# Rows of 512 elements for the gated activation, and 64 bytes between x and the weights in SBUF

## The chip, the cores and the metric

The kernel runs on one core of a Trainium2 chip. The metric is the device time of one execution in microseconds; before the change it is 534.3 us, the median of three runs (533.48 to 535.36). A measurement is compared with runs of the kernel before on the same chip.

## The reference

Banded attention over 8 images, 8 heads, 576 positions and 64 numbers per head; heads 0 to 3 see the last 32 positions, heads 4 to 7 every 32nd position. Its output, 4,608 tokens of 512 numbers, goes through a gated MLP. Cut to what matters here:

```python
h = np.maximum(x @ w_in, 0.0)                      # 4608 x 512 times 512 x 1024
hp = pad(h, 1 position on either side)
conv_out = sum(conv_w[k] * hp[:, k:k + S, :] for k in range(3))
gate = 1.0 / (1.0 + np.exp(-conv_out))
return (h * gate @ w_out)                          # 4608 x 1024 times 1024 x 512
```

## The kernel before

**Precision.** Both products of the MLP are made of three passes each: every operand is kept as a high and a low part (xh and xl, wih and wil, gh and gl, woh and wol, all of type fp32r), and high times high, high times low and low times high are added in PSUM. The weights arrive as 64-bit numbers and are taken apart on the chip in the first 85 us (`convert`, `from_f64`, lines 330 to 422).

**Tiling.** The 4,608 tokens are nine groups of N = 512 tokens (g = 0 to 8). The MLP works feature by feature: features lie on the 128 partitions, tokens along the row.

- `mm1` (line 607), the first product: for each of 8 blocks f of 128 hidden features it adds 4 blocks c of 128 inputs, three matmuls each (xh with wih, xh with wil, xl with wih). Every matmul streams a row of 512 tokens through a 128x128 block of weights: 96 matmuls in a group.
- `conv_gate` makes of the result, on ScalarE, VectorE and GpSimd, the gated activation of block f, and `split` (lines 430 to 435) stores it as the high part gh (ScalarE, line 431) and the low part gl (VectorE or GpSimd, line 434), in row f of two tiles of 8 rows.
- `mm2` (line 667), the second product: for each of 4 blocks m of 128 outputs it adds 8 blocks f, three matmuls each (woh with gh, wol with gh, woh with gl), 512 tokens wide: 96 in a group. The last group has one token more on its row (n = 513) and is done in two halves of 256 and 258 columns: 192 matmuls.

Between the matmuls of the MLP stand those of attention: scores (lines 449 and 458) and values (line 514) of four pairs of heads for every further image. The values of an image go into xh and xl, which hold 1,024 tokens, two groups, in 4 rows (c).

**Order.** All work is written down as operations with an engine, an expected duration, a due time and the keys that they read and write, in a `Plan`. `order` plays this plan through once, engine by engine, and the operations are then issued in the order found. The keys decide what waits in the plan: `("g", f)` with `"h"` or `"l"` stands for row f of gh or gl. On the chip, waits are set by the bytes that instructions touch.

**Layout.** The tiles of a pool lie one behind the other in SBUF in the order in which they are asked for, each at the next multiple of 32 bytes in every partition. The sizes per partition: xh, xl, wih, wil, woh and wol 16,384 bytes each (rows of 4,096 bytes for x and w_in, of 2,048 for w_out; a block of weights is 512 bytes wide), gh and gl 8 rows of N + 32 = 544 elements, 17,408 bytes. The attention buffers (qk, v, t, tt, mx, sm, twice) come behind wol, then the masks and smaller tiles.

Of the kernel before, what the change touches and what calls it, by code (L numbers as in the profile page):

```python
# [10 lines left out]
F32 = _mybir.dt.float32  # L11
F32R = _mybir.dt.float32r
BF16 = _mybir.dt.bfloat16
I32 = _mybir.dt.int32
# [6 lines left out]
P = 128  # L21
W = 32
# [42 lines left out]
class Plan:  # L65
# [6 lines left out]
    def op(self, engine, dur, at, fn, reads=(), writes=(), chain=(), table=None, lock=False, key=None):  # L72
        i = len(self.ops)
        deps = set(chain)
        for k in reads:
            if k in self.last_write:
                deps.add(self.last_write[k])
        for k in writes:
            deps.update(self.readers.get(k, ()))
            if k in self.last_write:  # L80
                deps.add(self.last_write[k])
        for k in reads:
            self.readers.setdefault(k, set()).add(i)
        for k in writes:
            self.last_write[k] = i
            self.readers[k] = set()
        deps.discard(i)
        self.ops.append((engine, dur, at, fn, deps, table, lock))
        return i
# [160 lines left out]
def tile_banded_attention_gated_mlp(ctx, tc, qkT, vw, w_in, conv, w_out, masks_in, picks_in, eye_in, out):  # L250
    nc = tc.nc
# [4 lines left out]
    NF, NM = w_in.shape[0], w_out.shape[0] // 2  # L256
# [4 lines left out]
    N = 4 * P  # L261
    NG = B * S // N
    HPS = [0, 2, 1, 3]
    V, A, G, T, Q = "dve", "act", "pool", "pe", "dma"
    plan = Plan()
    op = plan.op

    const = ctx.enter_context(tc.tile_pool(name="const", bufs=1))
    xh = const.tile([P, NC, 2 * N], F32R, name="xh")
    xl = const.tile([P, NC, 2 * N], F32R, name="xl")  # L270
    wih = const.tile([P, NC, FF], F32R, name="wih")
    wil = const.tile([P, NC, FF], F32R, name="wil")
    gh = const.tile([P, NF, N + 32], F32R, name="gh")
    gl = const.tile([P, NF, N + 32], F32R, name="gl")
    woh = const.tile([P, NF, DM], F32R, name="woh")
    wol = const.tile([P, NF, DM], F32R, name="wol")

    def attention_buffers(pool, i):
        qk = pool.tile([P, S + SP], F32, name=f"qk{i}")
# [5 lines left out]
    NB = 2  # L285
    buffers = [attention_buffers(const, i) for i in range(NB)]
    masks = const.tile([P, 2, 2, NBLK * 64], BF16, name="masks")
    picks = const.tile([P, 2, W], BF16, name="picks")
    eye = const.tile([P, P], F32, name="eye")
    eyer = const.tile([P, P], F32R, name="eyer")  # L290
    negr = const.tile([P, P], F32R, name="negr")
    cw = const.tile([P, 3 * NF], F32, name="cw")
    mlp = ctx.enter_context(tc.tile_pool(name="mlp", bufs=1))
    NHB, NPM = 3, 4
# [1 line left out]
    misc = mlp.tile([P, 2 * NHB * L], F32, name="misc")  # L296
    hs = [misc[:, L * i:L * i + L] for i in range(NHB)]
    cs = [misc[:, L * (NHB + i):L * (NHB + i) + L] for i in range(NHB)]
    carry = mlp.tile([P, NF, 2], F32, name="carry")
    psum = ctx.enter_context(tc.tile_pool(name="psum", bufs=1, space=PSUM))  # L300
    psR = psum.tile([P, 2048], F32, name="r")
    psM = [psum.tile([P, 512], F32, name=f"m{i}") for i in range(NPM)]
# [1 line left out]
    words = [const.tile([P, 8 * P, 2], I32, name=f"ws{i}") for i in range(NWS)]  # L304
    wa = [const.tile([P, 8 * P], I32, name=f"wa{i}") for i in range(NWA)]
    wl = [const.tile([P, 8 * P], F32R, name=f"wl{i}") for i in range(NWL)]
    small = const.tile([P, W], F32, name="small")
    diag = const.tile([P, 2 * NBLK, W], F32, name="diag")
    cwords = const.tile([P, 3 * NF, 2], I32, name="cwords")
    cwa = const.tile([P, 3 * NF], I32, name="cwa")  # L310
    cwt = const.tile([P, 3 * NF], I32, name="cwt")

# [114 lines left out]
        seen.add(a)  # L427
        return [("W", "in", b) for b in range(2)]

    def split(hi, lo, src, at, skey, key, e, ta, tv, tg, lock):  # L430
        op(A, ta, at, lambda: nc.scalar.copy(hi(), src), [skey], [(key, "h")])  # L431
        eng = nc.gpsimd if e == "p" else nc.vector
        op(G if e == "p" else V, tg if e == "p" else tv, at,
           lambda: eng.tensor_tensor(out=lo(), in0=src, in1=hi().bitcast(F32), op=ALU.subtract),  # L434
           [skey, (key, "h")], [(key, "l")], lock=lock or e == "p")

    def probabilities(n, at):
        i, hp = slot(n), HPS[n % NHP]
# [177 lines left out]
    def conv_gate(g, f, at, early, ps, kp):  # L616
        hi = state["h"] % NHB
        state["h"] += 1
        h, c_ = hs[hi], cs[hi]
        n = N + (g == NG - 1)  # L620
        cg = FIRST_CG if early else CG
        cut = 64 * g if 0 < g else None
        sg = FIRST_SPLIT_G[f] if early else SPLIT_G[f]
        op(A, 0.596, at + cg[2], lambda: nc.scalar.activation(out=h[:, 2:N + 2], in_=ps, func=AF.Relu), [kp], [("h", hi)])  # L624
        if g:
            op(G, 0.295, at + cg[0], lambda: nc.gpsimd.tensor_copy(out=h[:, 0:2], in_=carry[:, f, :]), [("carry", f)], [("h0", hi)], lock=True)  # L626
        if g < NG - 1:
            op(G, 0.3, at + cg[1], lambda: nc.gpsimd.tensor_copy(out=carry[:, f, :], in_=h[:, N:N + 2]), [("h", hi)], [("carry", f)], lock=True)
        kh = [("h", hi), ("h0", hi)]
        kc = ("c", hi)  # L630
        new = old(L * (NHB + hi), L)
        w0, w1, w2 = (cw[:, k * NF + f:k * NF + f + 1] for k in range(3))
        if not early or FIRST_SCALE[f] == "a":
            op(A, 0.725, at + cg[3], lambda: nc.scalar.activation(out=c_[:, :n], in_=h[:, 1:n + 1], func=AF.Copy, scale=w1),  # L634
               kh + ["cw"], [kc] + new)
        else:
            op(V, 0.4, at + cg[3], lambda: nc.vector.tensor_scalar(out=c_[:, :n], in0=h[:, 1:n + 1], scalar1=w1, scalar2=None,
                                                         op0=ALU.mult), kh + ["cw"], [kc] + new, lock=True)
        for k, wk in ((0, w0), (2, w2)):
            skip = n if cut is None else cut + 1 - k // 2  # L640
            for a, z in ((0, skip), (skip + 1, n)):
                if z > a:
                    op(V, 0.11 + 0.00117 * (z - a), at + cg[4] + 0.4 * k, lambda k=k, wk=wk, a=a, z=z: nc.vector.scalar_tensor_tensor(  # L643
                        out=c_[:, a:z], in0=h[:, a + k:z + k], scalar=wk, in1=c_[:, a:z],
                        op0=ALU.mult, op1=ALU.add), kh + [kc], [kc], lock=True)
        op(A, 0.63, at + cg[5], lambda: nc.scalar.activation(out=c_[:, :n], in_=c_[:, :n], func=AF.Sigmoid), [kc], [kc], table=1)  # L646
        ge = G if early and FIRST_GATE[f] == "p" else V
        op(ge, 0.69 if ge == V else 1.28, at + cg[6], lambda: (nc.vector if ge == V else nc.gpsimd).tensor_tensor(  # L648
            out=c_[:, :n], in0=h[:, 1:n + 1], in1=c_[:, :n], op=ALU.mult), kh + [kc], [kc], lock=True)
        split(lambda: gh[:, f, :n], lambda: gl[:, f, :n], c_[:, :n], at + cg[7], kc, ("g", f), sg, 0.62, 0.69, 1.2, True)  # L650

    def mm2(g, m, at):
        ms = slice(m * P, m * P + P)
        oi = (state["h"] + (0, 1, 2, 2)[m]) % NHB
        o, ko = (hs[oi], [("h", oi), ("h0", oi)]) if m == 2 else (cs[oi], [("c", oi)])
        cuts = [0, N] if g < NG - 1 else [0, N // 2, N + 1]
        first, last = N * g - 1, m == NM - 1
        for t, (a0, z) in enumerate(zip(cuts, cuts[1:])):
            x = z - a0 & 1
            mi = state["m"] % NPM  # L660
            state["m"] += 1
            ps = psM[mi][:, x:z - a0 + x]
            for f in range(NF):
                def products(f=f, ps=psM[mi][:, :z - a0 + x], tok=slice(a0 - x, z)):
                    n = 0
                    for a, y in ((woh, gh), (wol, gh), (woh, gl)):
                        nc.tensor.matmul(ps, a[:, f, ms], y[:, f, tok], start=(f == 0 and n == 0),  # L667
                                         stop=(f == NF - 1 and n == 2))
                        n += 1
                i = 2 * m + f // 4  # L670
                state["last"] = op(T, 0.697 if z - a0 == N else 0.36, at + 3 * t, products,
                                   [(("g", f), "h"), (("g", f), "l"), (("wo", i), "h"), (("wo", i), "l")], [("M", mi)], [])
            op(A, 0.59 if z - a0 == N else 0.38, at + 3 * t + 3, lambda ps=ps, a0=a0, z=z: nc.scalar.copy(o[:, a0:z], ps), [("M", mi)],  # L673
               ko)
            if g < NG - 1 or last:
                s = 1 if g == 0 else a0
                op(Q, 256 // len(cuts[1:]), at + 6, lambda s=s, z=z: nc.sync.dma_start(out=out[ms, first + s:first + z], in_=o[:, s:z]), ko, [])
        if g == NG - 1 and not last:
            op(Q, 256, at + 6, lambda: nc.sync.dma_start(out=out[ms, first:first + N + 1], in_=o[:, 0:N + 1]), ko, [])
# [8 lines left out]
    with tc.manual_schedule():  # L688
# [27 lines left out]
        for g in range(NG):  # L716
# [12 lines left out]
            if g + 1 < B:  # L729
                for j in range(NHP):  # L730
                    n = (g + 1) * NHP + j + 1
# [66 lines left out]
```

## Time and profile before

| what | us |
| --- | --- |
| median of three runs | 534.3 (533.48 to 535.36) |
| the profiled execution, its whole time | 535.48 |
| its span, first to last instruction | 533.3 |
| mean granted TensorE clock in it | 0.987 of full |
| TensorE in use | 511.3 |
| weight loads (PEld), beside it | 410.0 |
| VectorE, ScalarE, GpSimd in use | 362.4, 320.0, 118.8 |

The page gives times in us, and mean durations in ns. PE is TensorE's matmuls, PEld its weight loads. The duration of a matmul in the trace overlaps the next one's, so the time that one costs is read from start to start, or from a stretch of many in the chain of work that ended last. In that chain a row is the start, the length, the engine, what is written, the line, and the number of instructions.

### The profile page before, as it was taken

Reading aid. Unit: us, or ns where it says so; the run is one execution under the profiler, and the core shown is the slowest. Engines: PE = TensorE matmul, PEld = TensorE weight load, DVE = VectorE, ACT = ScalarE, POOL = GpSimd, SP = SyncE. Lnnn points to the kernel's source line nnn. Section 1 sums busy time; section 2 is a strip of 40 time slices with the busy share of each in tenths; the row PEclk is TensorE's granted clock in tenths of the full one; section 3 lists DMA queues with packets and bytes.
Section 4 is the critical chain, followed back from the end, with each engine's and each line's share of the span. In section 5 each row is a group of like instructions: output and inputs, shape, how many; then the busy total and the mean of one; then the engine's idle time right before and its main releaser. Section 6 shows DMA issues by size and latency. Waiting matters only on the chain.

```text
span 533.3 us, 16633 instructions
## 1 busy us (share of the span) xinstructions
PE 511.3 (96%) x7352; PEld 410.0 (77%) x7352; DVE 362.4 (68%) x639; ACT 320.0 (60%) x492; POOL 118.8 (22%) x197
## 2 busy tenths in 40 slices
PE   3787999999999999999999999999999999999997
PEld 3555677778877887788778877887788778888897
DVE  3967799866786568747975785688658845832840
ACT  2453786856674667556837776577547755733841
POOL 0111201532222112212131321222212221320210
PEclk9887999999999999999999999999999999999999
DMA  8655522343034403520334044303440101001001
GB/s 284 250 164 203 187 79 77 123 165 100 2 124 136 126 0 124 171 92 7 122 106 153 1 122 136 128 0 109 139 138 1 33 7 74 1 9 71 0 32 48
DMA packets 17639, 51.30 MB, mean 96 GB/s; under 512 B 2208, under 2 KB 3360, under 8 KB 17568
## 3 DMA queue, kind: packets, MB, share of 16 engines
q1 hardware_dynamic: 17568, 50.25, 28.0%
q8 instruction: 57, 0.93, 0.7%
q14 instruction: 14, 0.11, 0.1%
HBM read 40.80 MB, written 9.44 MB: 94 GB/s over the span
## 4 chain that ended last, share of the span: by engine, by line
PE 93%; ACT 2%; DVE 2%; DMA 1%; issue 1%; SPq 1%; ACTq 0%
PE m L667 39%; PE m L607 37%; PE r L514 6%; PE r L458 4%; PE m L411 2%; PE r L449 1%; DMA misc<-in_dram 1%; PE r L569 1%; PE m L412 1%; PE m L413 1%; ACT xh L549 0%; ACT wa L334 0%; ACT wih L400 0%; PE r L486 0%; DVE t L471 0%
## 5 line engine op out<-in xcount | busy, mean ns | idle before, releaser
L643 DVE SCALAR_TENSOR_TENSOR misc<-misc,cw 128x512 f32<-128x512 f32 (+29 forms) x256 | 127.9, 547 | 35.9 <-ACT misc L634 35.3
L667 PE MATMUL m<-gh,woh 128*128 128x512 f32 (+2 forms) x320 | 123.8, 387 | 0.0
L667 PE MATMUL m<-gl,woh 128*128 128x512 f32 (+2 forms) x320 | 118.8, 371 | 0.0
L667 PE MATMUL m<-gh,wol 128*128 128x512 f32 (+2 forms) x320 | 118.6, 371 | 0.0
L607 PE MATMUL m<-xh,wih 128*128 128x512 f32 x288 | 113.3, 393 | 0.0
L607 PE MATMUL m<-xh,wil 128*128 128x512 f32 x288 | 112.5, 391 | 0.0
L607 PE MATMUL m<-xl,wih 128*128 128x512 f32 x288 | 112.4, 390 | 0.0
L492 POOL TENSOR_TENSOR t<-t,sm 128x640 f32<-128x640 f32 x31 | 45.4, 1463 | 118.2 <-DVE sm L476 105.9
L667 PEld LDWEIGHTS m<-gh,woh 128*128 128x128 f32 x320 | 60.1, 188 | 12.4
L624 ACT ACTIVATE misc<-m 128x512 f32<-128x512 f32 x72 | 42.9, 596 | 43.2 <-PE m L607 41.5
L667 PEld LDWEIGHTS m<-gl,woh 128*128 128x128 f32 x320 | 60.1, 188 | 11.1
L667 PEld LDWEIGHTS m<-gh,wol 128*128 128x128 f32 x320 | 60.2, 188 | 9.1
L607 PEld LDWEIGHTS m<-xh,wih 128*128 128x128 f32 x288 | 54.1, 188 | 11.7 <-issue 0.2
L607 PEld LDWEIGHTS m<-xl,wih 128*128 128x128 f32 x288 | 54.2, 188 | 11.4
L607 PEld LDWEIGHTS m<-xh,wil 128*128 128x128 f32 x288 | 54.2, 188 | 11.3
L634 ACT ACTIVATE misc<-misc,cw 128x512 f32<-128x512 f32 (+1 forms) x70 | 50.6, 724 | 11.3 <-DVE gl L434 5.2
L648 DVE TENSOR_TENSOR misc<-misc 128x512 f32<-128x512 f32 (+1 forms) x69 | 47.8, 693 | 13.2 <-ACT misc L646 12.9
L646 ACT ACTIVATE misc<-misc 128x512 f32<-128x512 f32 (+1 forms) x72 | 44.6, 627 | 15.0 <-DVE misc L643 14.3
L431 ACT CAST gh<-misc 128x512 fp32r<-128x512 f32 (+1 forms) x72 | 44.2, 618 | 13.0 <-DVE misc L648 11.3
L673 ACT COPY misc<-m 128x512 f32<-128x512 f32 (+2 forms) x40 | 21.6, 546 | 47.9 <-PE m L667 47.3
L626 POOL COPY misc<-carry 128x2 f32<-128x2 f32 x64 | 19.1, 298 | 131.6 <-DVE misc L648 93.8
L470 DVE TENSOR_REDUCE mx<-r 128x10 f32<-128x640 f32 x32 | 26.3, 820 | 31.4 <-PE r L458 31.4
(84 smaller groups left out, 586.3 us busy)
## 6 DMA issues: line engine op xcount, KB each, us to landing
qk<-in_dram SPq DMA_DIRECT2D x32, 592.0 KB, 3.9
v<-in_dram SPq DMA_DIRECT2D x32, 384.0 KB, 3.4
ws<-in_dram SPq DMA_DIRECT2D x14, 512.0 KB, 4.7
out_dram<-misc SPq DMA_DIRECT2D x28, 256.0 KB, 3.1
misc<-in_dram SPq DMA_DIRECT2D x2, 512.0 KB, 5.8
out_dram<-misc SPq DMA_DIRECT2D x4, 255.5 KB, 3.7
out_dram<-misc SPq DMA_DIRECT2D x3, 256.5 KB, 2.0
masks<-in_dram SPq DMA_DIRECT2D x2, 160.0 KB, 2.6
```

The source lines that it names most:

```text
L431: op(A, ta, at, lambda: nc.scalar.copy(hi(), src), [skey], [(key, "h")])
L470: op(V, 0.826, at + offset[0], lambda: nc.vector.tensor_reduce(out=mx, in_=p3, axis=AX.X, op=ALU.max), ks, [("mx", i)])
L492: op(G, 1.28, at + offset[5], lambda: nc.gpsimd.tensor_tensor(out=t, in0=t, in1=sm.unsqueeze(2).to_broadcast([P, 2 * NBLK, 64]), op=ALU.mu ...
L514: nc.tensor.matmul(psV[64 * h:64 * h + 64, o:o + n_], v[W * c:W * c + W, h, j], tt[W * c:W * c + W, 64 * NBLK * h + a:64 * NBLK * h + z], ...
L607: nc.tensor.matmul(ps, a[:, c, fs], x[:, c, N * x0:N * x0 + N], start=(n == 0 and m == 0), stop=(n == NC - 1 and m == 2))
L624: op(A, 0.596, at + cg[2], lambda: nc.scalar.activation(out=h[:, 2:N + 2], in_=ps, func=AF.Relu), [kp], [("h", hi)])
L634: op(A, 0.725, at + cg[3], lambda: nc.scalar.activation(out=c_[:, :n], in_=h[:, 1:n + 1], func=AF.Copy, scale=w1), kh + ["cw"], [kc] + new)
L643: op(V, 0.11 + 0.00117 * (z - a), at + cg[4] + 0.4 * k, lambda k=k, wk=wk, a=a, z=z: nc.vector.scalar_tensor_tensor(out=c_[:, a:z], in0=h[ ...
L646: op(A, 0.63, at + cg[5], lambda: nc.scalar.activation(out=c_[:, :n], in_=c_[:, :n], func=AF.Sigmoid), [kc], [kc], table=1)
L648: op(ge, 0.69 if ge == V else 1.28, at + cg[6], lambda: (nc.vector if ge == V else nc.gpsimd).tensor_tensor(out=c_[:, :n], in0=h[:, 1:n + ...
L667: nc.tensor.matmul(ps, a[:, f, ms], y[:, f, tok], start=(f == 0 and n == 0), stop=(f == NF - 1 and n == 2))
L673: op(A, 0.59 if z - a0 == N else 0.38, at + 3 * t + 3, lambda ps=ps, a0=a0, z=z: nc.scalar.copy(o[:, a0:z], ps), [("M", mi)], ko)
```

## The change

It moves tiles in SBUF and changes the distance between rows of gh and gl. The operations of the first eight groups stay as they are.

- A row of gh and gl is 512 elements in all groups but the last, and 514 in the last one (`row`); the two become flat tiles of 8 x 514 elements, 16,448 bytes.
- carry, 64 bytes, is put between xl and wih. woh and wol go ahead of gh. Between gh and gl go eye, eyer, negr, picks, small and cwords, together 1,984 bytes.
- As a row of the last group overlaps two of the group before, its `split` also writes the key of row f + 1 in the plan (`over`).

Distances from the beginning of xh, in bytes per partition:

| tile | before | after |
| --- | --- | --- |
| xh, xl | 0, 16,384 | 0, 16,384 |
| carry | (behind misc) | 32,768 |
| wih, wil | 32,768, 49,152 | 32,832, 49,216 |
| gh, gl | 65,536, 82,944 | 98,368, 116,800 |
| woh, wol | 100,352, 116,736 | 65,600, 81,984 |
| first attention buffer | 133,120 | 133,248 |

```diff
     xh = const.tile([P, NC, 2 * N], F32R, name="xh")
     xl = const.tile([P, NC, 2 * N], F32R, name="xl")
+    carry = const.tile([P, NF, 2], F32, name="carry")
     wih = const.tile([P, NC, FF], F32R, name="wih")
     wil = const.tile([P, NC, FF], F32R, name="wil")
-    gh = const.tile([P, NF, N + 32], F32R, name="gh")
-    gl = const.tile([P, NF, N + 32], F32R, name="gl")
     woh = const.tile([P, NF, DM], F32R, name="woh")
     wol = const.tile([P, NF, DM], F32R, name="wol")
+    gh = const.tile([P, NF * (N + 2)], F32R, name="gh")
+    eye = const.tile([P, P], F32, name="eye")
+    eyer = const.tile([P, P], F32R, name="eyer")
+    negr = const.tile([P, P], F32R, name="negr")
+    picks = const.tile([P, 2, W], BF16, name="picks")
+    small = const.tile([P, W], F32, name="small")
+    cwords = const.tile([P, 3 * NF, 2], I32, name="cwords")
+    gl = const.tile([P, NF * (N + 2)], F32R, name="gl")
...
-    def split(hi, lo, src, at, skey, key, e, ta, tv, tg, lock):
-        op(A, ta, at, lambda: nc.scalar.copy(hi(), src), [skey], [(key, "h")])
+    def split(hi, lo, src, at, skey, key, e, ta, tv, tg, lock, over):
+        op(A, ta, at, lambda: nc.scalar.copy(hi(), src), [skey], [(k, "h") for k in [key] + over])
         eng = nc.gpsimd if e == "p" else nc.vector
         op(G if e == "p" else V, tg if e == "p" else tv, at,
            lambda: eng.tensor_tensor(out=lo(), in0=src, in1=hi().bitcast(F32), op=ALU.subtract),
-           [skey, (key, "h")], [(key, "l")], lock=lock or e == "p")
+           [skey, (key, "h")], [(k, "l") for k in [key] + over], lock=lock or e == "p")
...
-        split(lambda: gh[:, f, :n], lambda: gl[:, f, :n], c_[:, :n], at + cg[7], kc, ("g", f), sg, 0.62, 0.69, 1.2, True)
+        over = [("g", f + 1)] if n > N and f + 1 < NF else []
+        split(lambda: row(gh, g, f)[:, :n], lambda: row(gl, g, f)[:, :n], c_[:, :n], at + cg[7], kc, ("g", f), sg, 0.62, 0.69, 1.2, True, over)
+
+    def row(y, g, f):
+        pitch = N if g < NG - 1 else N + 2
+        return y[:, pitch * f:pitch * f + pitch]
...
-                        nc.tensor.matmul(ps, a[:, f, ms], y[:, f, tok], start=(f == 0 and n == 0),
+                        nc.tensor.matmul(ps, a[:, f, ms], row(y, g, f)[:, tok], start=(f == 0 and n == 0),
```

The other lines of the diff take the moved tiles out of their old places.

More of the change, by code (lines that the diff above doesn't have):

```diff
@@ L287, in tile_banded_attention_gated_mlp @@
     masks = const.tile([P, 2, 2, NBLK * 64], BF16, name="masks")
[L288 to L291, printed above, removed]
     cw = const.tile([P, 3 * NF], F32, name="cw")
@@ L298, in tile_banded_attention_gated_mlp @@
     cs = [misc[:, L * (NHB + i):L * (NHB + i) + L] for i in range(NHB)]
-    carry = mlp.tile([P, NF, 2], F32, name="carry")
     psum = ctx.enter_context(tc.tile_pool(name="psum", bufs=1, space=PSUM))
@@ L306, in tile_banded_attention_gated_mlp @@
     wl = [const.tile([P, 8 * P], F32R, name=f"wl{i}") for i in range(NWL)]
-    small = const.tile([P, W], F32, name="small")
     diag = const.tile([P, 2 * NBLK, W], F32, name="diag")
-    cwords = const.tile([P, 3 * NF, 2], I32, name="cwords")
     cwa = const.tile([P, 3 * NF], I32, name="cwa")
```

## The prediction

> **What bounds the kernel now.** I read the page's engine table and slices first, then the chain of work that ended last, then single stretches of that chain.
>
> ```profile
> span 533.3 us, 16633 instructions
> PE 511.3 (96%) x7352; PEld 410.0 (77%) x7352; DVE 362.4 (68%) x639; ACT 320.0 (60%) x492; POOL 118.8 (22%) x197
> PE   3787999999999999999999999999999999999997
> PEclk9887999999999999999999999999999999999999
> PE 93%; ACT 2%; DVE 2%; DMA 1%; issue 1%; SPq 1%; ACTq 0%
> PE m L667 39%; PE m L607 37%; PE r L514 6%; PE r L458 4%; PE m L411 2%; PE r L449 1%; DMA misc<-in_dram 1%; PE r L569 1%; PE m L412 1%; PE m L413 1%; ACT xh L549 0%; ACT wa L334 0%; ACT wih L400 0%; PE r L486 0%; DVE t L471 0%
> ```
>
> From the fifth slice on TensorE is in use without a gap and its granted clock is full. It makes 93% of the chain; 37% of the span is the first product (L607, x times w_in) and 39% the second (L667, gated activation times w_out). So what a matmul of these two lines takes from its start to the start of the next, its pace, goes into the time nearly one for one. How many there are is in the groups by shape:
>
> ```profile
> L607 PE MATMUL m<-xh,wih 128*128 128x512 f32 x288 | 113.3, 393 | 0.0
> L667 PE MATMUL m<-gh,woh 128*128 128x512 f32 x256 | 105.8, 413 | 0.0
> L607 PEld LDWEIGHTS m<-xh,wih 128*128 128x128 f32 x288 | 54.1, 188 | 11.7 <-issue 0.2
> ```
>
> Each line has three such groups, of equal count: 3 x 288 = 864 matmuls in the first product, 3 x 256 = 768 with 512 columns in the second (the last group of tokens has 192 narrower ones besides). Their 393 and 413 ns overlap; the pace has to be read from long unbroken stretches of the chain:
>
> ```profile
> 436.05 5.08 PE m L667 x21
> ...
> 465.70 19.45 PE m L667 x84
> 485.15 21.81 PE m L607 x96
> 506.96 22.80 PE m L667 x192
> ```
>
> The second product goes at 19.45 / 84 = 231.5 ns, the first at 21.81 / 96 = 227.2 ns, although both take 512 columns against a 128x128 weight. Work of other engines beside it is not the reason, since there is less of it in the slower stretch. The columns are the window, PE, PEld, DVE, ACT, POOL (busy us and count), clock, DMA:
>
> ```profile
> 465.80:484.90 19.10, 19.10 (x84) 15.50 (x83) 5.87 (x10) 5.84 (x10) 3.84 (x6) 1.00 0.11 41
> 485.30:506.90 21.60, 21.60 (x97) 17.86 (x96) 15.16 (x21) 15.17 (x26) 3.76 (x6) 1.00 0.04 13
> ```
>
> The next weights load while a row streams through (PEld is busy 15.50 of 19.10 us), and what differs between the lines is where the two lie. Before, xh, xl, wih and wil are 16,384 bytes each, one behind the other, so an x row and any weight block are a multiple of 512 bytes apart. A row of gh has 544 elements, 2,176 bytes, so row f lies 128 f modulo 512 from its weights: 0, 128, 256, 384, and again. That this matters shows in blocks of the second product between two pieces of attention. By the program's order the block at 208.96 stays in rows 4 and 0 (distance 0), the one at 163.12 in rows 6 and 2 (256), the one at 171.11 in row 7 (384), and the one at 167.11 goes through rows at all four distances:
>
> ```profile
> 163.12 2.94 PE m L667 x12
> 167.11 2.98 PE m L667 x12
> 171.11 2.99 PE m L667 x12
> 208.96 2.95 PE m L667 x12
> ```
>
> Start by start, the ends of the blocks at 256 and 0, and that at 384:
>
> ```profile
> 164.54 0.39 PE L667 MATMUL m<-gh,woh 128*128 128x512 f32 x1
> ...
> 165.67 0.39 PE L667 MATMUL m<-gl,woh 128*128 128x512 f32 x1
> ...
> 171.38 0.39 PE L667 MATMUL m<-gh,wol 128*128 128x512 f32 x1
> 171.60 0.40 PE L667 MATMUL m<-gl,woh 128*128 128x512 f32 x1
> ...
> 172.07 0.40 PE L667 MATMUL m<-gh,wol 128*128 128x512 f32 x1
> ...
> 173.71 0.40 PE L667 MATMUL m<-gl,woh 128*128 128x512 f32 x1
> ...
> 210.61 0.39 PE L667 MATMUL m<-gh,wol 128*128 128x512 f32 x1
> ...
> 211.52 0.39 PE L667 MATMUL m<-gl,woh 128*128 128x512 f32 x1
> ```
>
> At distances 0 and 256 the pace settles to that of the first product: from 210.61 to 211.52 are four steps of 228 ns, from 164.54 to 165.67 five of 226. At 384 it does not: from 172.07 to 173.71 are seven steps of 234 ns. So distance 0 has a steady pace, into which a block falls after some five matmuls, and a change to a row at 128 or 384 throws it out again.
>
> **The change, part by part.** No instruction, wait or transfer is added or taken away up to the last group; addresses move. Laid out in order, wih begins 32,832 bytes behind xh, 64 modulo 512 (before: 32,768, that is 0). gh begins 32,768 behind woh, and gl 18,432 = 36 x 512 behind gh; with rows of 512 elements (2,048 bytes) every row of g is then 0 modulo 512 from its weights.
>
> Second product, 768 matmuls, distance 128 f becomes 0. In the unbroken stretch and the 21 at 436.05, 105 matmuls can go from 231.5 to 227.2: 0.45 us. The rest stands in some 50 blocks between attention pieces (scores and values of four pairs of heads in each of seven images are 56 pieces, a few of which stand in the first product), which go from 2.98 to the 2.95 us of the block at distance 0, in which its start out of step is contained: 50 x 0.03 = 1.5 us. Together about 1.9 us. Lower end: half of the blocks' part and the long stretch, 1.2 us. Upper end: all 768 at 227.2, 768 x 4.3 ns = 3.3 us.
>
> Last group, 192 matmuls at 22.80 / 192 = 119 ns: rows of 514 elements, so the distance is 8 f (0 to 56 bytes) and not 128 f. If that does for half a row what it does for a row, 2% of 22.8 us at most, 0.45 us; since the distances are not quite 0, and could as well be bad ones, I take 0, with 0.45 either way.
>
> First product, 864 matmuls, distance 0 becomes 64: one nanosecond of pace is 0.86 us. No row of before shows an odd multiple of 64. The nearest rows are 227.2 ns at distance 0 and 234 at 128 or 384. The lower bound is the shortest step in the rows above, 0.22 us (171.38 to 171.60): 864 x 7.2 ns = 6.2 us less. The upper bound is 234 ns kept throughout: 864 x 6.8 = 5.9 us more. I take 227.2, no difference: it is the value at the nearest distance on one side (256 behaves as 0 does), 64 bytes away; but 128 is just as near on the other, so this is the weak term.
>
> The Trainium skill, "TensorE: Matmul & The Clock Gate", section "Step-by-step: what each phase is for", says that TensorE has two independent read ports, and that loading the next weights takes no bandwidth from the running matmul. By that rule no distance would matter and the sum would be 0. The 234 against 226 ns above speak against it. The same page (section "Wait — 56ns, not 53.3ns?") gives N/2.4 + 2.5 ns between warm matmuls, 215.8 for 512 columns; no row here is that short, and if 64 bytes brought it, an estimate from that page would be 864 x 11.4 ns = 9.8 us less.
>
> Other moves: the gate tiles of the last group write over parts of rows f and f + 1 of the group before, so the planner makes them wait for both, and one row's subtraction for that of the next. The second product of the group before ends at 485.15, before the first of these writes. The subtractions of the last group (L434), one each 2.7 us (12 x 227 ns), are:
>
> ```profile
> L434 DVE TENSOR_TENSOR gl<-misc,gh x5: 686/695/697, 493.2 to 512.7; 128x513 fp32r<-128x513 f32 x5
> L434 POOL TENSOR_TENSOR gl<-misc,gh x3: 1098/1100/1235, 499.0 to 513.5; 128x513 fp32r<-128x513 f32 x3
> ```
>
> The last on DVE ends at 513.4 and the last on POOL starts at 513.5: already one after the other, cost 0. Without that cover it would be one POOL subtraction, 1.1 us. qk, v, t and tt move together and keep their distances. picks, the unit matrices and small move against what they meet: L411 to L413, L449 and L569 together are 6% of the chain, 32 us, mostly at full tilt only in the first 85 us; at the 3% seen above that is 1 us at the very most either way, and I take 0.
>
> Sum: -1.9 us. The profiled execution ran 535.48 us (span 533.3 and 2.2 around it), 1.2 above the median of the three runs, 534.3; its 535.48 becomes 533.6, the median 532.4.
>
> **The rivals.** *The first product falls out of step* (the other side). At 64 it has no steady pace and goes as the second does now, at 231.5 ns: 864 x 4.3 = 3.7 us more, less the 1.9 won: 536.1; at 234 ns 5.9 more: 538.3. It costs more than the change wins from 227.2 + 1.9 / 0.864 = 229.4 ns on. For it: three of the four distances modulo 512 known here are 0, 128 and 384 (256 being like 0), and only one kind of them holds a steady pace. Against it: 64 is no nearer to the bad ones than to the good ones.
>
> *The first product gets faster.* If the cost of a row comes from where it meets the weight load, 64 may be better than 0. At 0.22 us it gives 6.2 us, with the 1.9 a time of 526.2; half of that, 529.3. For it: steps of 0.22 do occur, so 226 is no floor. Against it: none repeats.
>
> *The distance has no part in it.* The second product is slower for another reason, its three operands' order or its output; the change then does nothing, 534.3. For it: the rows at distances 128 and 384 are also other rows of data. Against it: the same line in the same order goes at 226 in one row and 234 in another. The skill's rule of independent ports, quoted above, would give this result.
>
> **How the numbers follow.** The forecast (second product wins, first unchanged) 0.37, its own range 531.0 to 533.5; first product out of step 0.28; first product faster 0.23; no effect 0.12. About 0.3%, 1.6 us, is what a measurement of this kernel can tell from no change, so faster begins at 532.7. The forecast splits, 0.24 faster and 0.13 same; the faster case is 0.23 faster; the one without effect 0.10 same and 0.02 slower; the one out of step 0.26 slower and 0.02 same. Together faster 0.47, same 0.25, slower 0.28. The range goes from the first product's lower bound to its upper one, 526.2 to 538.3, and leaves out 5 in 100 on either side.
>
> **What the profile of after would show.** For the second product: the stretch of 84 matmuls at 465 us takes 19.1 us instead of 19.45, and the blocks of 12 take about 2.95. For the first: the 96 matmuls of a group take 21.8 us if nothing changes, 22.2 or more if it falls out of step, 21.1 or less if 64 is the better distance. For the last group, 22.8 us. PEld's 188 ns and the counts stay as they are, and so does the order of instructions. The prediction is wrong if the 96 matmuls move by more than 0.2 us, or if the 84 stay at 19.45.

## The result, and the profile after

The change makes the kernel slower: 538.31 us against 534.09 (medians of 14 runs each on the same chip), ratio 1.007 with a 95% interval of 1.0054 to 1.0086, that is 3.7 us with 2.9 to 4.6. The ratio is that of the means; the medians themselves lie 4.2 us apart. The profiled execution of after took 538.82 us, its span is 536.7.

The page of after, engine table, clock and the chain's shares by line (`mm2`'s matmul is now line 672):

```profile
span 536.7 us, 16633 instructions
PE 515.1 (96%) x7352; PEld 410.0 (76%) x7352; DVE 362.5 (68%) x639; ACT 319.7 (60%) x492; POOL 118.7 (22%) x197
PEclk9887999999999999999999999999999999999999
PE 93%; ACT 2%; DVE 2%; DMA 1%; issue 1%; SPq 1%; ACTq 0%
```

Nothing but PE has moved: the same number of instructions on every engine, the same clock, the other engines busy as long as before to 0.3 us. The long stretches of the chain that ended last say where the time lies. Of after:

```profile
229.82 22.40 PE m L607 x96
...
284.14 22.40 PE m L607 x96
...
468.72 19.06 PE m L672 x84
487.78 22.40 PE m L607 x96
510.18 22.90 PE m L672 x192
```

The second product now goes at 19.06 / 84 = 226.9 ns (before 231.5). The first goes at 22.40 / 96 = 233.3 ns (before 227.2). The two have changed places, and the first has more matmuls: 864 against 768. In the chain's shares to a tenth of a percent, before and after (one view each, the line cut off by the view at its end):

```profile
by line: PE m L667 39.5%; PE m L607 36.9%; PE r L514 5.9%; PE r L458 4.3%; PE m L411 2.4%; PE r L449 1.5%; DMA misc<-in_dram 1.2%; issue 1.0%; PE r L569 0.6%; PE m L412 0.6%; PE m L413 0.6%; ACT xh L549 0.4%; ACT wa L334 0.4%; ACT wih L400 
```

```profile
by line: PE m L672 39.0%; PE m L607 37.6%; PE r L514 5.9%; PE r L458 4.3%; PE m L411 2.5%; PE r L449 1.4%; DMA misc<-in_dram 1.0%; issue 1.0%; PE r L569 0.6%; PE m L413 0.6%; PE m L412 0.6%; ACT xh L549 0.4%; ACT wa L334 0.4%; ACT wih L400 
```

The first product has 37.6% of 536.7 = 201.8 us after and 36.9% of 533.3 = 196.8 before, 5.0 us more. The second has 209.3 after and 210.7 before, 1.4 less. Together 3.6 us, and the spans differ by 3.4.

Start by start, the timeline of after shows the first product's new steady pace, 1.64 us from 487.85 to 489.49 in seven steps, 234 ns:

```profile
487.85 0.39 PE L607 MATMUL m<-xh,wil 128*128 128x512 f32 x1
488.09 0.39 PE L607 MATMUL m<-xl,wih 128*128 128x512 f32 x1
...
489.49 0.39 PE L607 MATMUL m<-xl,wih 128*128 128x512 f32 x1
```

The cost isn't transient: the stretch holds this pace, just as the 22.40 us of the whole group say.

### The profile page after: what moved, and what is told of

Read it like the earlier page. It is cut to its first block, busy times and chain, and to the rows that moved or that the text cites. A ratio compares the mean times of both kernels' runs of the same rounds, so it can differ in the third digit from the quotient of the medians.

```text
span 536.7 us, 16633 instructions
## 1 busy us (share of the span) xinstructions
PE 515.1 (96%) x7352; PEld 410.0 (76%) x7352; DVE 362.5 (68%) x639; ACT 319.7 (60%) x492; POOL 118.7 (22%) x197
## 4 chain that ended last, share of the span: by engine, by line
PE 93%; ACT 2%; DVE 2%; DMA 1%; issue 1%; SPq 1%; ACTq 0%
PE m L672 39%; PE m L607 38%; PE r L514 6%; PE r L458 4%; PE m L411 2%; PE r L449 1%; DMA misc<-in_dram 1%; PE r L569 1%; PE m L413 1%; PE m L412 1%; ACT xh L549 0%; ACT wa L334 0%; ACT wih L400 0%; PE r L486 0%; DVE t L471 0%
## 5 line engine op out<-in xcount | busy, mean ns | idle before, releaser
L643 DVE SCALAR_TENSOR_TENSOR misc<-misc,cw 128x512 f32<-128x512 f32 (+29 forms) x256 | 126.9, 542 | 36.9 <-ACT misc L634 36.5
L607 PE MATMUL m<-xh,wih 128*128 128x512 f32 x288 | 114.8, 399 | 0.0
L607 PE MATMUL m<-xh,wil 128*128 128x512 f32 x288 | 114.0, 396 | 0.0
L607 PE MATMUL m<-xl,wih 128*128 128x512 f32 x288 | 114.0, 396 | 0.0
```

Source lines behind the costliest of these rows:

```text
L607: nc.tensor.matmul(ps, a[:, c, fs], x[:, c, N * x0:N * x0 + N], start=(n == 0 and m == 0), stop=(n == NC - 1 and m == 2))
```

## The experiments

The theory: while a row streams, the weights of the next matmul load, and the distance between the two in SBUF, in bytes modulo 256, sets the pace. (A distance of 64 modulo 256 is 64 bytes more than some multiple of 256.) The rivals: the place of the weights or of the small tiles that moved, and not the distance; a property of the first product itself; or the distance to the row's own weights, which are loaded already, and not to the next ones. Where a kernel ran once, only the pace is read from it, in stretches that no pause interrupts; whole times are compared only for the two that were timed 12 and 7 times, against 17 runs of the kernel before on the same chip, since the times of the kernel before alone lie between 532.4 and 537.0 us in one set of runs.

**Rows of 512 alone.** The 64 bytes between x and w_in go away again: carry moves from between xl and wih to behind gl.

```diff
-    carry = const.tile([P, NF, 2], F32, name="carry")
...
     gl = const.tile([P, NF * (N + 2)], F32R, name="gl")
+    carry = const.tile([P, NF, 2], F32, name="carry")
```

> Rows of 512 elements for g as in the change, but no 64 bytes between x and the weights: x and w_in are again 0 modulo 512 apart, g and w_out 0. Theory (the distance between the streamed row and the weights that load beside it sets the pace): 96 matmuls of the first product in 21.8 us, 84 of the second in 19.05, the time 1.9 to 2.2 us below before, 532.0. Rival (place: both products take their pace from where the weights themselves lie, or the time comes from the small tiles that moved): the first product stays at 22.4 us, or the time stays above before, 536 or more.

```profile
461.92 19.04 PE m L672 x84
480.96 21.76 PE m L607 x96
502.72 22.89 PE m L672 x192
```

532.92 us against 534.33, ratio 0.9964 (0.9948 to 0.9981), 1.9 us less (1.0 to 2.8): faster than the kernel before, where the change was slower. The 84 and the 96 go at one pace now, 19.04 / 84 = 226.7 and 21.76 / 96 = 226.7 ns. The half of the change that was forecast as a gain is one, and the forecast 1.9 lies within what was measured.

**The 64 bytes alone**, in the kernel before.

```diff
+    carry = const.tile([P, NF, 2], F32, name="carry")
     wih = const.tile([P, NC, FF], F32R, name="wih")
...
-    carry = mlp.tile([P, NF, 2], F32, name="carry")
```

> The kernel before with only carry's 64 bytes put between xl and wih; rows of g keep 544 elements. Theory (distance): the 96 matmuls of the first product take 22.4 us as in the change, the 84 of the second 19.45 as before; 864 x 6.2 ns = 5.4 us more than before, 539.5. Rival (the small tiles that moved in the change, or rows of 512, made it slower): the first product stays at 21.8 and the time within 1 us of before.

```profile
473.09 19.46 PE m L667 x84
492.55 22.40 PE m L607 x96
514.95 22.81 PE m L667 x192
```

538.75 us against 534.33, ratio 1.0081 (1.0063 to 1.0099), 4.3 us more. The first product has the change's 22.40, the second and the last group are as before (19.45 and 22.80). The size is a little under the 5.4 us expected, which the interval (3.4 to 5.3) only just leaves out. The chain's shares say the same: the first product takes 37.3% of 541.3 = 201.9 us here, 5.1 more than before and inside the interval, so each of the 864 lost 5.9 ns in the mean and not 6.2.

**Everything 64 bytes further on**, so that w_in lies at the very address that it has in the change, at distance 0 from x.

```diff
+    pad_head = const.tile([P, 16], F32, name="pad_head")
     xh = const.tile([P, NC, 2 * N], F32R, name="xh")
```

> As rows_only, but 64 bytes of nothing ahead of xh, so that x, w_in, w_out and g all lie 64 bytes further on, w_in at the very address that it has in the change; the distances are 0. Theory (distance): 21.8 us for 96 of the first product, 19.05 for 84 of the second. Rival (the place of the weights modulo 512): 22.4 us for the first.

```profile
463.94 19.04 PE m L673 x84
482.98 21.76 PE m L608 x96
```

Both products go at 226.7 ns: it is the distance, not the place.

**Distances exchanged**: w_in 256 behind x, w_out 64 behind g. One piece of padding stands between xl and wih, the other between wol and gh.

```diff
+    pad_x = const.tile([P, 64], F32, name="pad_x")
...
+    pad_g = const.tile([P, 112], F32, name="pad_g")
```

> Distances exchanged: w_in lies 256 modulo 512 behind x, w_out 64 behind g. Theory (distance, with a period of 256 bytes, alike for both products): 96 of the first product in 21.8 us, 84 of the second in 233.4 x 84 = 19.6 us. Rival (the first product as such bears no shift, or the period is 512): 22.4 us for the first; or the second stays at 19.05.

```profile
465.58 19.61 PE m L674 x84
485.19 21.78 PE m L609 x96
```

Now the second product bears the 233.5 ns, the first goes at 226.9. It is not a property of the first product, and 256 is as good as 0. Which product is slow follows the padding.

**Is any distance better, and how far does 0 reach?** The same two paddings with other sizes, four kernels.

> Rows of 512 for g; w_in 128 modulo 512 behind x, w_out 32 behind g. Theory A (only multiples of 256 hold the pace of 226.7 ns, everything else goes at about 233): 96 of the first product in 22.3 to 22.5 us, 84 of the second in 19.5 to 19.65. Theory B (the pace falls or rises evenly between 0 and 64 bytes): 84 of the second at 230 ns, 19.3 us. Theory C (some distance is better than 0): below 19.0 for the 84 at 32.

```profile
470.14 19.59 PE m L674 x84
489.74 22.31 PE m L609 x96
```

> w_in 192 behind x, w_out 96 behind g. Theory A: 22.3 to 22.5 us for 96 of the first product, 19.5 to 19.65 for 84 of the second. Theory B (even between the known points, with a period of 256): 192 is 64 on the other side, 22.4; 96 lies between two points at 233, 19.6. Theory C: one of them below 21.7 or 19.0.

```profile
283.92 21.98 PE m L609 x96
468.29 19.68 PE m L674 x84
487.97 22.40 PE m L609 x96
```

> w_in 32 behind x, w_out 224 behind g (32 on the other side of a multiple of 256). Theory A: 22.3 to 22.5 and 19.5 to 19.65 us. Theory B: 230 ns in both, 22.1 and 19.3. Theory C: below 21.7 or 19.0. That the product has no part in it asks for 32 to give the same pace here in the first as in the second of the kernel with 128 and 32.

```profile
468.47 19.60 PE m L674 x84
488.07 22.39 PE m L609 x96
```

> w_in 320 behind x (64 more than 256), w_out 160 behind g. With a period of 256 bytes the first goes as at 64: 22.4 us for 96. With a period of 512 it may be anything, 21.8 included. The second at 160: Theory A and B 19.5 to 19.65, Theory C below 19.0.

```profile
470.59 19.60 PE m L674 x84
490.19 22.39 PE m L609 x96
```

No distance tried beats 0. In ns for one matmul: 32 gives 233.2 in either product, 64 and 320 give 233.3 and 233.2, 96 gives 234.3, 128 gives 232.4, 160 and 224 give 233.3. Theory B, a pace that rises evenly with the distance, is out: 32 bytes cost all that 64 do. The range of Theory A held but for 96, 0.03 us above it, and for 192: there the same 96 matmuls take 21.98 us (229.0 ns) in the group at 283.92 and 22.40 (233.3) in the one at 487.97. One distance can have two lasting paces. The first of these stretches comes behind attention, the second directly behind the second product, so what came before seems to decide; this was not tried.

**How exact must it be?** x rows begin 16 bytes further on, g rows 8, with the weights at a multiple of 256 as before.

```diff
-    xh = const.tile([P, NC, 2 * N], F32R, name="xh")
+    xh = const.tile([P, NC * 2 * N + 128], F32R, name="xh")[:, 4:4 + NC * 2 * N].rearrange("p (c n) -> p c n", c=NC)
...
-    gh = const.tile([P, NF * (N + 2)], F32R, name="gh")
+    gh = const.tile([P, NF * (N + 2) + 128], F32R, name="gh")[:, 2:2 + NF * (N + 2)]
```

> As rows_only, but x rows begin 16 bytes further on and g rows 8 bytes, the weights stay: x is 16 bytes and g 8 bytes ahead. If only an exact multiple of 256 settles at 226.7 ns: 96 of the first product at 22.2 to 22.5 us and 84 of the second at 19.4 to 19.65. If what counts is the block of 32 or 64 bytes that the row begins in: 21.8 and 19.05, as at 0.

```profile
469.04 19.62 PE m L672 x84
488.65 22.24 PE m L607 x96
```

Two elements are enough to lose the pace: 233.6 ns at 8 bytes, 231.7 at 16.

**Own weights or the next ones?** Rows of 528 elements in g and in w_out, so that a row is always 0 from its own weights, and 64 (another multiple of 64 where the order skips rows) from those that load during its last matmul, where the next row follows.

```diff
-    woh = const.tile([P, NF, DM], F32R, name="woh")
+    woh = const.tile([P, NF, DM + 16], F32R, name="woh")
...
-        pitch = N if g < NG - 1 else N + 2
+        pitch = N + 16
```

> As rows_only, but rows of g and of w_out both 528 elements: row f of g lies 0 modulo 512 from its own weights, and 64 from those of the rows next to it, so every third matmul, the last one of a row, streams while weights at another distance load. Theory N (what counts is the distance to the weights that load beside the row, those of the next matmul): the 84 of the second product do not settle, 19.3 to 19.5 us. Theory O (the distance to the row's own weights counts): 19.05 us. The first product, unchanged at 0, 21.8 us for 96.

```profile
464.78 19.44 PE m L672 x84
484.22 21.78 PE m L607 x96
506.00 22.58 PE m L672 x192
```

The control, with rows of w_out of 512:

> As rows_only, but rows of g of 528 elements against rows of w_out of 512: row f lies 64 f modulo 512 from its weights. Both theories: 84 of the second product at 19.4 to 19.6 us, since the distance changes with every row and only rows 0 and 4 are at a multiple of 256; 21.8 us for 96 of the first. It is the control for rows of 528 in both.

```profile
465.97 19.49 PE m L672 x84
485.46 21.78 PE m L607 x96
507.24 22.72 PE m L672 x192
```

With its own weights at 0 throughout, the second product still goes at 231.4 ns, nearly what the control gives (232.0), not at 226.7. So 0 from its own weights is not enough. The reading that fits the theory is that the distance to the weights that load beside the row counts, and that at most one matmul in three at the wrong distance keeps the stretch from settling. Another is left: at the same places the streamed row jumps by 64 modulo 256 from the row before it, and the weights likewise, and no run changes the one without the other. The 231.4 ns are also the pace of the kernel before (231.5), where rows changed the distance.

## Why the prediction was wrong

**Which term.** The step that failed is the one on the first product: "I take 227.2, no difference". It put the term at nothing; measured were 233.3 ns, 5.0 us more by the chain's shares, and this turned a forecast gain of 1.9 us into a loss of 3.7. The prediction's own sign of being wrong, the 96 matmuls off by more than 0.2 us, came with 22.40 for 21.81. The rival "the first product falls out of step" is what happened, in its place (864 matmuls at 64 bytes) and at its price: 538.3 at 234 ns, measured 538.31, a hair outside the range, whose upper end was that price. That the two agree to 0.01 us is luck: the price was 5.9 where 5.0 was measured, and the gain taken off it 1.9 where 1.4 was, so 4.0 in all against the measured 3.7. Nor is the rival's picture quite what happened. At 64 the first product does not lose its steady pace but keeps another one, the seven even steps of 234 ns above.

**Why it was taken wrongly.** The argument was that 64 lies as near to a good distance as to a bad one. That treats the pace as a smooth function of the distance, which no row showed. The traces now show 0 and 256 as the only distances with the pace of 226.7 among those tried, and 8 bytes off as already bad. The rows of before held a better hint: the second product passed through 0, 128, 256 and 384, and only at multiples of 256 did a steady 226 appear. The slower pace is the general case and the better one the exception; the rival should have had the larger chance. The upper bound, 234 from the row at 384, was the right row for the price.

**What held.** The second product: the stretch of 84 was to take 19.1 and took 19.06, blocks of 12 were to take about 2.95. Two blocks of the chain of after, one that settles early and one that settles late, and the 21 that took 5.08 before, are

```profile
95.01 2.94 PE m L672 x12
99.00 2.97 PE m L672 x12
...
438.54 5.01 PE m L672 x21
```

Rows of 512 alone are worth 1.9 us in the timed runs, the sum's figure. By the chain's shares the line of the second product gained a little less, 1.4 us in the change and 1.7 with rows of 512 alone (39.5% of 529.2 = 209.0 against 210.7), where a share is rounded to some 0.3 us. Two long stretches gave 0.46 of it (0.39 and 0.07), as summed, and the last group took 0.1 back, so the blocks between attention gave about 1.0 to 1.3 us: the 50 x 0.03 = 1.5 of the sum was somewhat too large. In the change the second product starts out of step where it follows the first without a pause, but that costs hundredths: the 84 take 19.06 us against 19.04. The last group, taken as 0 with 0.45 either way, went from 22.80 to 22.90. That 8 f is no good distance shows in the kernel with rows of 528 in both, where most of the matmuls are at 0 and the last group took 22.58. The planner's added waits cost nothing that the profile shows, and the small tiles' moves neither: the shares of L411 to L413, L449 and L569 agree to 0.1% each.

**The rule that was weighed.** The Trainium skill ("TensorE: Matmul & The Clock Gate", "Step-by-step: what each phase is for") has loading the next weights take no bandwidth from the running matmul. The runs differ: with the same instructions, 226.7 ns or 233.3, by the distance between the rows and the weights. The measurement decides. The Trainium skill's N/2.4 + 2.5 ns (same page, "Wait — 56ns, not 53.3ns?"), by which 512 columns would take an estimated 215.8, was reached at no distance tried.

## What to carry to other kernels

Where a product is bound by TensorE and every matmul loads weights, look at where streamed rows and the next weights lie in SBUF: in this kernel a distance of exactly 0 modulo 256 bytes, kept from one matmul to the next, was worth 6.6 ns of 233, and a shift of 8 bytes lost it. Read the pace from start to start in a stretch without pauses; busy times and mean durations hide it. When a new layout goes to a point that the trace has never shown, and the good points seen so far are exact ones, expect the common, bad pace there.

## What was not expected of the hardware

Two paces come back again and again: 226.7 ns (21.76 / 96) and about 233.3 (22.40 / 96), 6.6 ns apart, hold through whole groups, the better one also where other engines are busy beside it (in the kernel before, VectorE was busy 15.16 us of 21.60 in a stretch at nearly that pace). Between them stand 231.7 at 16 bytes and 232.4 at 128, above them 234.3 at 96. At 192 bytes one and the same loop had two, 229.0 and 233.3, in one execution. Behind a pause a stretch at distance 0 reaches its pace after some five to ten matmuls: the block at 95.01 gets there after five and takes 2.94 us, the one at 99.00 after ten and takes 2.97. Why multiples of 256 are the ones that settle stays open: the runs show the dependence on the distance between rows and weights, not what in SBUF or TensorE makes it.
